# A recurrence and a top-1 mixture of experts on one core: weight loads spread over the first scatters, two chunks in the first routing group, throttles kept in the planner alone

## The chip, the cores and the metric

One core of a Trainium2 chip runs the whole program. The metric is the device time in microseconds (us) of one execution, lower is better. Three runs of the kernel before gave 561.56, 562.37 and 565.24 us, the median is 562.37 us.

## The reference

The inputs are `x` and `f_logit`, both (4, 5056, 256) in float32, a vector `lower_bound` of 256, eight expert embeddings and the two weight matrices of eight experts. First a gated recurrence runs along the 5056 steps of each of the four sequences; then each of the 20224 rows that come out goes to the one expert whose embedding is nearest, and is scaled by that expert's probability.

```python
sig = 1.0 / (1.0 + np.exp(-f_logit))
f = lower_bound + (1.0 - lower_bound) * sig
h = f[:, t] * h + (1.0 - f[:, t]) * x[:, t]      # for each step t; y[:, t] = h
...
logits = xn @ en.T / tau                          # xn, en: rows divided by their norms
expert_idx = np.argmax(logits, axis=1)
out[mask] = gate_w[mask, None] * (np.maximum(y[mask] @ w1[e], 0.0) @ w2[e])
```

## The kernel before, in words

**Stages.** The 20224 rows are cut into 40 chunks of 512 (the last has 256). A chunk is loaded by SP (`load`, L573, three buffers each for `f_logit`, called `fin`, and `x`, called `xin`). `F_` (L774) transposes `fin` on TensorE (L782), ScalarE makes the tanh `th` (L793) and the gate `fg` (L799), once for each half `dh` of the 256 columns. `X_` (L806) transposes `xin` (L816); VectorE multiplies it by the gate (L824) and runs the recurrence as a scan along the row (L840), into `hb`. `Y_` (L847) squares it and turns it back into rows in the tile `Yt`, in chunks below 14 by TensorE transposes (L886) and a copy (L897), later by a bf16 copy `hbf` (L861) and a DMA transpose.

**Routing.** Chunks are put into groups (`groups`, L767): before, chunks 0 and 1 are a group each, then two chunks each up to chunk 37, then 38 and 39 alone; 22 groups. `route_` (L934) computes the logits of a group on TensorE (L945, L949), copies them (L961), transposes them (L967), and a string of small VectorE operations (L976 to L1042) finds the expert and, with some matmuls (L1013 to L1026), the row's slot in a table sorted by expert. `gate_` (L1048) computes the probability with some fifteen more small VectorE operations (L537 to L1095). Both strings are as long for a group of one chunk as for a group of two (with one chunk a memset, L1001, comes on top). Then GpSimd (POOL) scatters the rows, 128 at a time, into the DRAM tensor `XsScratch` (L1109): four indirect DMAs for each chunk, 158 in all.

**Experts.** After some groups `update_` (L1123) writes a table that says which 256 rows of one expert a tile takes (`ups`, L1524: a list of group numbers). `tile_` (L1318) computes one of 81 tiles: it loads the rows, runs the first matmuls (L1434, 32 weight blocks from `wall` in SBUF at a register's address), ReLU on ScalarE and VectorE (L1455, L1460) into `hT`, the second matmuls (L1482), scales the two halves (L1497 on ScalarE, L1501 on VectorE, into `osb`, six buffers) and writes them with two indirect DMAs from POOL (L1507). A tile's matmuls wait for all weights that it might need: tiles 0 to 3 for the loads 0 to 7, tiles 4 to 7 for 0 to 11, the others for all 16 (`FEW`, L397, and `wr`, L1419).

**Weights.** `wload` (L751) asks from POOL for one of 16 loads, 1 MB in float32 read and 512 KB in bf16 written, two for each expert. A load waits until the load two before it has landed. All 16 are handed to the planner with chunk 0 and its priority (L1557).

**Order.** Nothing is ordered by hand. `Prog.op` (L62) records each operation with an engine, a cost, and its dependences: `deps` become semaphore waits where another engine or a DMA is concerned, `order` only places one after the other on an engine. `Prog.schedule` (L129) then plays a list schedule with these costs and writes down one fixed order for each engine; `resolve` (L290) and `emit` put in the waits. Lower `prio` goes first: a chunk's work has the chunk's number, a tile's 10000 and more, so that tiles fill the places in which the plan sees TensorE free. PSUM's eight banks are given out by the same plan (`Hold`). Some dependences are no data dependences but throttles: `F_`'s transposes wait (`deps`, L790) for the readers of `th` and of the same `fg` buffer two chunks ago, `X_`'s transposes read `fg` by their record (L822), though they touch only `xin` and a bank; likewise `Y_`, the logits, the turned rows of the first tiles and the first matmuls list the readers of a buffer that a later copy will write. In the planner VectorE may hold a long operation back for up to 250 ns when an operation of an early chunk is about to be ready (`soon`, L192, for priorities up to 3). The ReLUs carry the tag `mid`; with all routing work planned, the second matmuls that read them are planned 2600 ns later. A scatter and the writes of all but the last four tiles are `paced`: POOL waits for a TensorE step that the plan saw done by then.

```python
if o.dma is not None:
    bus = max(bus, free[e]) + o.nbytes / self.DMA_RATE      # the plan's DMA: one bus in order
    o.end = max(bus, free[e]) + self.DMA_FIX
```

Of the kernel before, what the change touches and what calls it, by code (L numbers as in the profile page):

```python
# [17 lines left out]
class Op:  # L18
    __slots__ = (
        "eng", "fn", "deps", "order", "dma", "val", "know", "used", "cost", "nbytes", "prio",  # L20
        "idx", "start", "end", "tag", "astart", "aend", "hold", "quiet", "late", "paced",
# [13 lines left out]
class Prog:  # L35
# [26 lines left out]
    def op(self, eng, fn, cost, r=(), w=(), x=(), deps=(), order=(), dma=None, nbytes=0, prio=None, tag="", chain=True, h=None):  # L62
# [52 lines left out]
        o.deps, o.order = list(need.values()), list(order.values())  # L115
        self.ops.append(o)
        return o

    def filler(self, q, n):
        f = Op()  # L120
        f.eng, f.dma, f.nbytes, f.cost = "pe", None, 0, n * self.UNIT
        f.val, f.know, f.used, f.tag = 0, None, False, ""
        f.prio, f.idx, f.quiet, f.late, f.paced, f.hold = -9, len(self.ops), True, False, False, ()
        f.deps, f.order = [self.warm_on], []
        f.fn = lambda e: self.warm(e, q, n)
        self.ops.append(f)
        return f

    def schedule(self, first, caps):  # L129
# [3 lines left out]
        for o in self.ops:  # L133
            left[id(o)] = len(o.deps) + len(o.order)
            for d in o.deps:
                succ[id(d)].append((o, True))
            for d in o.order:
                succ[id(d)].append((o, False))
# [34 lines left out]
        while True:  # L173
# [17 lines left out]
            if e == "dve" and avail[e] and avail[e][0][2].cost > 400:  # L191
                soon = min(  # L192
                    (w for w in wait[e] if w[0] <= s + 250 and w[1] < avail[e][0][0] and w[1] <= 3),
                    default=None, key=lambda w: w[:3],
                )
# [177 lines left out]
def bass_hgrn_recurrence__then__cosine_router_kernel(  # L373
# [41 lines left out]
    with ExitStack() as es:  # L415
# [335 lines left out]
        def wload(i, c):  # L751
# [6 lines left out]
            else:  # L758
# [4 lines left out]
                deps=[pr.writer.get(("w", i - 2))], nbytes=1 << 20, prio=c,  # L763
            )


        groups = [[0], [1]] + [[2 * g, 2 * g + 1] for g in range(1, (NCH - 2) // 2)] + [[NCH - 2], [NCH - 1]]  # L767
# [6 lines left out]
        def F_(c):  # L774
            q, nb = c % NXI, nof(c) // P
            n = nof(c)
            for dh in range(DT):
                h = Hold("a")

                def fn(e, dh=dh, h=h):  # L780
# [9 lines left out]
                    deps=[pr.readers.get(("th", dh), []), pr.readers.get(("fg", c % 2, dh), [])],  # L790
# [15 lines left out]
        def X_(c):  # L806
# [4 lines left out]
            for dh in range(DT):  # L811
# [10 lines left out]
                pe(fn, 110 * nb, r=[("xin", q), "ident", ("fg", c % 2, dh)], h=h)  # L822
# [24 lines left out]
        def Y_(c):  # L847
# [32 lines left out]
            for hf in range(nb // 2):  # L880
                h = Hold("a")

                def fn(e, hf=hf, h=h):
# [10 lines left out]
                    deps=pr.readers.get(("Yt", bi % NY, k_, hf), []),  # L894
# [39 lines left out]
        def route_(g):  # L934
# [7 lines left out]
            def lg(e):  # L942
# [13 lines left out]
                lg, 1760, h=hl, deps=pr.readers.get(("lgS", g % 2), []),  # L956
# [361 lines left out]
        def tile_(j, u, g, n):  # L1318
# [57 lines left out]
            if j < NPE:  # L1376
                hy = Hold("a")

                def turn(e):
# [14 lines left out]
                    deps=pr.readers.get(("ys", qy, 0), []), prio=EVP(pr.prio),  # L1394
# [29 lines left out]
            for mp in range(2):  # L1424
                hh = (Hold("m"), Hold("m"))

                def mm1(e, mp=mp, hh=hh):
# [20 lines left out]
                    mm1, 1000 if last else 874, r=yk + wr, h=hh, order=[prev],  # L1448
                    deps=pr.readers.get(("hT", qh, 2 * mp), []) + pr.readers.get(("hT", qh, 2 * mp + 1), []),
                )  # L1450
                for m, h in ((2 * mp, hh[0]), (2 * mp + 1, hh[1])):
                    o = hT[qh][:, 2 * m : 2 * m + 2, :].rearrange("p f c -> p (f c)")
                    if m % 2 == 0:
                        act(
                            lambda e, o=o, h=h: e.activation(o, bank[h.b][:], AF.Relu), 512,  # L1455
                            h=h, w=[("hT", qh, m)], prio=EVP(pr.prio), tag="mid",
                        )
                    else:
# [4 lines left out]
                            512, h=h, w=[("hT", qh, m)], prio=EVP(pr.prio), tag="mid",  # L1463
# [10 lines left out]
            for m in range(4):  # L1474
                if split:
                    at = [(kf, m // 2) for kf in range(4 * (m % 2), 4 * (m % 2) + 4)]
                else:
                    at = [(kf, s) for kf in (2 * m, 2 * m + 1) for s in range(2)]
# [45 lines left out]
        ups = [3, 4, 5, 7, 9, 11, 13, 15, 17, 18, 19, 20] + [NG - 1, NG - 1]  # L1524
# [10 lines left out]
        YBOOST = 1.5  # L1535

# [12 lines left out]
        for c in range(NCH):  # L1549
# [6 lines left out]
            if c == 0:  # L1556
                for i in range(2 * E):  # L1557
                    wload(i, c)
            if c == 1:
                late_constants()  # L1560
            if c in last_of:
# [3 lines left out]
                if g == batches[bi][-1]:  # L1565
                    gate_(bi)
                for u, at in enumerate(ups):
                    if at == g:
                        update_(u, g, u == len(ups) - 1)
# [63 lines left out]
```

## Time and profile before

| | us |
|---|---|
| median of three runs (561.56 to 565.24) | 562.37 |
| the profiled execution | 565.46 |
| its span, first to last instruction | 563.7 |
| TensorE (PE) busy | 475.2 |
| VectorE (DVE) busy | 359.5 |
| GpSimd (POOL) busy | 331.9 |
| ScalarE (ACT) busy | 321.1 |

The span's share that an engine is busy is a mean over stages with different limits. PE is the matmuls, PEld the loads of their stationary side, which overlap with them. POOL's busy time is the issue of indirect DMAs, nearly 1 us each, and leaves out 0.3 us between one and the next. "PEclk" is the clock that was granted to TensorE, as a share of full speed. The DMA share is a mean over 16 engines and comes out a little over 1 where all are busy.

### The profile page before, as it was taken

To read this page: it belongs to the slowest core of one execution; us is meant where nothing else is said; L and a number is where in the kernel's file an instruction comes from. 1 tells how busy PE (TensorE), PEld (TensorE's weight loads), DVE (VectorE), ACT (ScalarE), POOL (GpSimd) and SP (SyncE) were. 2 spreads that over 40 slices of the span, in tenths; PEclk is the share of its full clock that TensorE was granted. 3 is DMA by queue.
4 is the path that set the end of the run, shared out by engine and by line. 5 is a ranking of instruction groups with operands and counts; after the bars stand their busy time and mean duration, and the time that the engine had idled before them with its cause. 6 is when DMAs were issued, how large, how long until landed. Compare 5 with 4: busy or idle time off the path is not lost. (4 is left out here: it accounts for less than half of the span.)

```text
span 563.7 us, 12407 instructions
## 1 busy us (share of the span) xinstructions
PE 475.2 (84%) x4106; PEld 382.8 (68%) x4106; DVE 359.5 (64%) x1075; ACT 321.1 (57%) x573; POOL 331.9 (59%) x388
## 2 busy tenths in 40 slices
PE   7796778979798789887887988888988897978994
PEld 4474557757577567656765657777777776867894
DVE  7869978877787667875877876533444343443452
ACT  4878768877787566757776753333333332333342
POOL 6164565655665565564666665656665666655555
PEclk8969988998998889999999999999999999999998
DMA  8999999999999788879896543353343433444422
GB/s 243 302 311 313 318 254 311 287 254 219 206 234 241 202 205 190 238 172 219 221 241 133 117 92 99 113 127 105 100 110 95 110 88 100 106 109 101 106 65 74
DMA packets 119681, 100.49 MB, mean 178 GB/s; under 512 B 96884, under 2 KB 98687, under 8 KB 119616
## 3 DMA queue, kind: packets, MB, share of 16 engines
q1 hardware_dynamic: 101664, 59.38, 42.5%
q0 software_dynamic: 16224, 40.26, 26.2%
q8 instruction: 36, 0.59, 0.5%
q10 hardware_dynamic: 1728, 0.01, 0.2%
q14 instruction: 29, 0.24, 0.2%
HBM read 59.21 MB, written 32.93 MB: 163 GB/s over the span
## 5 line engine op out<-in xcount | busy, mean ns | idle before, releaser
L1507 POOL DMA_INDIRECT out_dram<-osb,xm x162 | 160.7, 992 | 107.6 <-issue 34.0
L1109 POOL DMA_INDIRECT XsScratch<-Yt,sli x158 | 152.2, 963 | 105.6 <-issue 26.6
L1434 PE MATMUL bank<-ys,wall 128*128 128x256 bf16 (+1 forms) x1392 | 174.4, 271 | 19.1 <-issue 13.4
L1482 PE MATMUL bank<-wall,hT 128*128 x1296 | 172.8, 274 | 15.0 <-issue 12.6
L1460 DVE TENSOR_SCALAR hT<-bank 128x512 bf16<-128x512 f32 x162 | 108.4, 684 | 100.8 <-remote 46.0
L1434 PEld LDWEIGHTS bank<-ys,wall 128*128 x1392 | 147.5, 145 | 34.9 <-issue 24.7
L1455 ACT ACTIVATE hT<-bank 128x512 bf16<-128x512 f32 x162 | 94.0, 597 | 114.1 <-remote 49.5
L1482 PEld LDWEIGHTS bank<-wall,hT 128*128 128x128 bf16 x1296 | 124.4, 98 | 42.9 <-issue 23.0
L840 DVE TENSOR_TENSOR_SCAN hb<-fg,hb,bank 128x512 f32<-128x512 f32 (+4 forms) x78 | 95.9, 1236 | 0.1
L1501 DVE TENSOR_SCALAR osb<-bank,xm 128x256 f32<-128x256 f32 x81 | 38.8, 479 | 59.7 <-ACT osb L1497 32.6
L1497 ACT ACTIVATE osb<-bank,xm 128x256 f32<-128x256 f32 x81 | 38.4, 475 | 59.7 <-remote 17.4
L816 PE MATMUL bank<-ident,xin 128*128 128x128 f32 x316 | 53.2, 294 | 22.7 <-ACT fg L799 12.9
L799 ACT ACTIVATE fg<-th,cs 128x512 f32<-128x512 f32 (+1 forms) x80 | 64.4, 812 | 1.4 <-DVE cs L627 0.2
L816 PEld LDWEIGHTS bank<-ident,xin 128*128 128x128 f32 x316 | 37.7, 149 | 34.6 <-ACT fg L799 16.9
L824 DVE SCALAR_TENSOR_TENSOR bank<-fg,bank 128x512 f32<-128x512 f32 (+1 forms) x80 | 54.1, 680 | 9.6 <-PE bank L816 6.8
L793 ACT ACTIVATE th<-bank 128x512 f32<-128x512 f32 (+1 forms) x80 | 46.3, 592 | 22.7 <-PE bank L782 14.2
L782 PE MATMUL bank<-ident,fin 128*128 128x128 f32 x316 | 53.5, 300 | 4.5 <-DMA fin<-in_f_logit_dram 2.0
L782 PEld LDWEIGHTS bank<-ident,fin 128*128 128x128 f32 x316 | 40.4, 155 | 12.2 <-issue 4.5
L852 ACT ACTIVATE sq<-hb 128x1024 f32<-128x1024 f32 (+1 forms) x40 | 41.8, 1045 | 2.0 <-DVE hb L840 1.6
L945 PE MATMUL bank<-hb,eT 128*8 128x512 f32 (+1 forms) x160 | 41.7, 599 | 0.3 <-issue 0.3
L949 PE MATMUL bank<-sq,onesf 128*1 128x512 f32 (+1 forms) x160 | 41.5, 597 | 0.0
L861 ACT ACTIVATE hbf<-hb 128x512 bf16<-128x512 f32 x50 | 31.4, 629 | 4.7 <-DVE hb L840 4.2
(139 smaller groups left out, 305.3 us busy)
## 6 DMA issues: line engine op xcount, KB each, us to landing
fin<-in_f_logit_dram SPq DMA_DIRECT2D x39, 512.0 KB
xin<-in_x_dram SPq DMA_DIRECT2D x39, 512.0 KB
wall<-in_moe_w_dram POOLq DMA_DIRECT2D x16, 512.0 KB, 10.6
out_dram<-osb,xm POOLq DMA_INDIRECT x162
XsScratch<-Yt,sli POOLq DMA_INDIRECT x158
ys<-XsScratch SPq DMA_TRANSPOSE x81
xm<-XsScratch SPq DMA_DIRECT2D x75, 2.0 KB
osb<-XsScratch SPq DMA_DIRECT2D x6, 136.0 KB
```

The lines of the kernel that those rows point to most:

```text
L782: i = e.transpose(bank[h.b][:, b : nb * P : nb], fin[q][:, b, dh * P : (dh + 1) * P], ident[:],)
L793: lambda e, dh=dh, h=h: e.activation(th[dh][:, 0:n], bank[h.b][:, 0:n], AF.Tanh, scale=0.5),
L799: lambda e, dh=dh: e.activation(fg[c % 2][:, dh, 0:n], th[dh][:, 0:n], AF.Identity, bias=cs[:, dh, 0:1], scale=cs[:, dh, 1:2],),
L816: i = e.transpose(bank[h.b][:, b : nb * P : nb], xin[q][:, b, dh * P : (dh + 1) * P], ident[:],)
L824: lambda e, dh=dh, h=h: e.scalar_tensor_tensor(out=bank[h.b][:, 0:n], in0=fg[c % 2][:, dh, 0:n], scalar=1.0, in1=bank[h.b][:, 0:n], op0=AL ...
L840: lambda e, dh=dh, s0=s0, s1=s1, init=init, h=h: e.tensor_tensor_scan(hb[c % NH][:, dh, s0:s1], fg[c % 2][:, dh, s0:s1], bank[h.b][:, s0:s ...
L1109: lambda e, j=o + j, i=o + k_ * 4 + b: e.indirect_dma_start(out=Xs[:, :], out_offset=bass.IndirectOffsetOnAxis(ap=sli[y][:, j : j + 1], axis=0
L1434: i = e.matmul(bank[hh[f // 2].b][:, at : at + R_], wall[:, bass.ds(a1[j, s][(4 * mp + f) * DT + kt] - WA - WREV, 2 * FT * P),].bitcast(BF ...
L1455: lambda e, o=o, h=h: e.activation(o, bank[h.b][:], AF.Relu), 512,
L1460: lambda e, o=o, h=h: e.tensor_scalar(o, bank[h.b][:], 0.0, None, op0=ALU.max),
L1482: i = e.matmul(po(s), hT[qh][:, kf, s * P : (s + 1) * P], wall[:, bass.ds(a2[j, s if last else 0][kf] - WA, 2 * D)].bitcast(BF16), start=( ...
L1507: lambda e, s=s: e.indirect_dma_start(out=out[:, :], out_offset=bass.IndirectOffsetOnAxis(ap=xm[qx][:, s, 1:2], axis=0), in_=osb[qo][:, s, :],
```

## The change

Six edits. (1) `op` takes a list `behind`: the planner counts it like `deps`, but no semaphore wait comes of it. The throttles named above move from `deps` to `behind`, and `X_`'s transposes no longer record `fg` as read. (2) Chunks 0 and 1 form one group; there are 21 groups, and `ups` is renumbered to the same chunks. (3) Six weight loads stay with chunk 0; the other ten are handed over two by two after the groups that end with chunks 3, 5, 7, 9 and 11, each ordered on POOL behind that group's last scatter. (4) `soon` takes priorities up to 5. (5) For the last two tiles the tag `mid` is gone, and the last tile's second half of first matmuls is ordered behind the second matmuls of the tile before. (6) The last tile's second matmuls alternate between its two halves instead of finishing the first half first.

```diff
         o.deps, o.order = list(need.values()), list(order.values())
+        o.behind = [q for q in flat(behind) if q is not o]
...
-            left[id(o)] = len(o.deps) + len(o.order)
-            for d in o.deps:
+            left[id(o)] = len(o.deps) + len(o.order) + len(o.behind)
+            for d in o.deps + o.behind:
                 succ[id(d)].append((o, True))
...
-                    (w for w in wait[e] if w[0] <= s + 250 and w[1] < avail[e][0][0] and w[1] <= 3),
+                    (w for w in wait[e] if w[0] <= s + 250 and w[1] < avail[e][0][0] and w[1] <= 5),
...
                 deps=[pr.writer.get(("w", i - 2))], nbytes=1 << 20, prio=c,
+                order=[pr.writer.get(("Xs", gof[c][0]))],
...
-        groups = [[0], [1]] + [[2 * g, 2 * g + 1] for g in range(1, (NCH - 2) // 2)] + [[NCH - 2], [NCH - 1]]
+        groups = [[2 * g, 2 * g + 1] for g in range((NCH - 2) // 2)] + [[NCH - 2], [NCH - 1]]
...
-                    deps=[pr.readers.get(("th", dh), []), pr.readers.get(("fg", c % 2, dh), [])],
+                    behind=[pr.readers.get(("th", dh), []), pr.readers.get(("fg", c % 2, dh), [])],
...
-                pe(fn, 110 * nb, r=[("xin", q), "ident", ("fg", c % 2, dh)], h=h)
+                pe(fn, 110 * nb, r=[("xin", q), "ident"], h=h, behind=[pr.writer[("fg", c % 2, dh)]])
...
-                    deps=pr.readers.get(("Yt", bi % NY, k_, hf), []),
+                    behind=pr.readers.get(("Yt", bi % NY, k_, hf), []),
...
-                lg, 1760, h=hl, deps=pr.readers.get(("lgS", g % 2), []),
+                lg, 1760, h=hl, behind=pr.readers.get(("lgS", g % 2), []),
...
-                    deps=pr.readers.get(("ys", qy, 0), []), prio=EVP(pr.prio),
+                    behind=pr.readers.get(("ys", qy, 0), []), prio=EVP(pr.prio),
...
-                    mm1, 1000 if last else 874, r=yk + wr, h=hh, order=[prev],
-                    deps=pr.readers.get(("hT", qh, 2 * mp), []) + pr.readers.get(("hT", qh, 2 * mp + 1), []),
+                    mm1, 1000 if last else 874, r=yk + wr, h=hh,
+                    order=[prev, last_mm[2] if mp and n == NM - 1 else None],
+                    behind=pr.readers.get(("hT", qh, 2 * mp), []) + pr.readers.get(("hT", qh, 2 * mp + 1), []),
...
-                            h=h, w=[("hT", qh, m)], prio=EVP(pr.prio), tag="mid",
+                            h=h, w=[("hT", qh, m)], prio=EVP(pr.prio), tag="mid" if n < NM - 2 else "",
...
-                    at = [(kf, m // 2) for kf in range(4 * (m % 2), 4 * (m % 2) + 4)]
+                    at = [(kf, m % 2) for kf in range(4 * (m // 2), 4 * (m // 2) + 4)]
...
-        ups = [3, 4, 5, 7, 9, 11, 13, 15, 17, 18, 19, 20] + [NG - 1, NG - 1]
+        ups = [2, 3, 4, 6, 8, 10, 12, 14, 16, 17, 18, 19] + [NG - 1, NG - 1]
...
+        WBEHIND = [(6, 1), (8, 2), (10, 3), (12, 4), (14, 5)]
...
             if c == 0:
-                for i in range(2 * E):
+                for i in range(WBEHIND[0][0]):
                     wload(i, c)
...
+                for n, (i0, at) in enumerate(WBEHIND):
+                    if at == g:
+                        for i in range(i0, WBEHIND[n + 1][0] if n + 1 < len(WBEHIND) else 2 * E):
+                            wload(i, c)
```

## Rows read from the trace of the kernel before

**Rows 1.** The page's slices: 40 equal parts of the span, busy tenths.

```profile
PE   7796778979798789887887988888988897978994
...
DVE  7869978877787667875877876533444343443452
...
DMA  8999999999999788879896543353343433444422
```

**Rows 2.** Stretches: PE, PEld, DVE, ACT, POOL busy us (instructions); PEclk, DMA share, GB/s.

```profile
48.00:94.00 46.00, 36.41 (x304) 27.11 (x303) 40.48 (x143) 35.73 (x58) 28.73 (x33) 0.89 1.02 296
94.00:108.00 14.00, 12.05 (x126) 9.72 (x124) 10.54 (x38) 11.71 (x23) 9.00 (x11) 1.00 1.08 280
108.00:333.00 225.00, 191.31 (x1665) 147.08 (x1664) 170.24 (x520) 159.91 (x282) 133.63 (x137) 0.97 0.85 205
333.00:490.00 157.00, 137.54 (x1171) 118.04 (x1170) 72.02 (x206) 55.75 (x113) 96.81 (x99) 1.00 0.39 102
490.00:553.00 63.00, 57.59 (x586) 51.71 (x584) 25.88 (x45) 22.58 (x46) 35.75 (x37) 1.00 0.42 98
```

**Rows 3.** TensorE in order of time (start, us, instruction): chunk 4, the first tile.

```profile
28.71 1.09 PE L816 MATMUL bank<-ident,xin 128*128 128x128 f32 x4 [1.99 <-DMA xin<-in_x_dram]
...
94.02 1.91 PE L1434 MATMUL bank<-ys,wall 128*128 128x256 bf16 x16
```

**Rows 4.** POOL in order of time: the last six writes, first and last.

```profile
553.80 0.98 POOL L1507 DMA_INDIRECT out_dram<-osb,xm  x1 [2.27 <-DVE osb L1501]
...
560.26 0.98 POOL L1507 DMA_INDIRECT out_dram<-osb,xm  x1 [0.30 <-issue]
```

**Rows 5.** VectorE in order of time, the first two routing rounds.

```profile
20.19 0.16 DVE L976 TENSOR_REDUCE rmax<-bank 128x4 f32<-128x32 f32 x1
...
22.67 0.19 DVE L1035 TENSOR_TENSOR slt<-bank,oh 128x32 f32<-128x32 f32 x1 [0.27 <-PE bank L1026]
...
23.31 0.69 DVE L824 SCALAR_TENSOR_TENSOR bank<-fg,bank 128x512 f32<-128x512 f32 x1
...
26.76 0.19 DVE L1035 TENSOR_TENSOR slt<-bank,oh 128x32 f32<-128x32 f32 x1 [0.58 <-PE bank L1026]
...
27.64 1.27 DVE L840 TENSOR_TENSOR_SCAN hb<-fg,hb,bank 128x512 f32<-128x512 f32 x1
...
29.12 0.14 DVE L1095 TENSOR_SCALAR Yt<-tokf 128x4 int32<-128x4 f32 x1
```

**Rows 6.** POOL in order of time: weight loads (L762) and scatters (L1109).

```profile
27.50 1.06 POOL L1109 DMA_INDIRECT XsScratch<-Yt,sli  x1 [6.94 <-DVE rs L1062]
...
45.30 0.58 POOL L762 DMA_DIRECT2D wall<-in_moe_w_dram  x1 [4.37 <-DMA wall<-in_moe_w_dram]
47.41 1.00 POOL L1109 DMA_INDIRECT XsScratch<-Yt,sli  x1 [1.52 <-DVE Yt L1095]
...
59.09 0.99 POOL L1109 DMA_INDIRECT XsScratch<-Yt,sli  x1 [0.63 <-PE bank L886]
...
101.14 0.58 POOL L762 DMA_DIRECT2D wall<-in_moe_w_dram  x1
...
122.13 0.96 POOL L1109 DMA_INDIRECT XsScratch<-Yt,sli  x1 [0.30 <-PE bank L816]
```

**Rows 7.** Groups: count, busy us, mean ns, idle us before them and what ended it.

```profile
L824 DVE SCALAR_TENSOR_TENSOR bank<-fg,bank 128x512 f32<-128x512 f32 (+1 forms) x80 | 54.1, 680 | 9.6 <-PE bank L816 6.8
```

**Rows 8.** TensorE's group of L816 from 48 to 108 us.

```profile
L816 PE MATMUL bank<-ident,xin 128*128 128x128 f32 x72 | 13.3, 315 | 9.9 <-ACT fg L799 9.1 <-issue 0.8
```

**Rows 9.** TensorE's groups from 108 to 333 us.

```profile
L1434 PE MATMUL bank<-ys,wall 128*128 128x256 bf16 x446 | 60.7, 283 | 7.3 <-issue 3.6 <-DVE osb L1501 2.4 <-DVE slt L1035 1.0
L816 PE MATMUL bank<-ident,xin 128*128 128x128 f32 x191 | 30.2, 281 | 8.7 <-ACT th L793 3.1 <-ACT fg L799 2.3 <-ACT hT L1455 1.8
L782 PE MATMUL bank<-ident,fin 128*128 128x128 f32 x184 | 29.7, 286 | 2.1 <-DVE hb L840 1.0 <-issue 0.8 <-DVE nr L1058 0.2
```

More of the change, by code (lines that the diff above doesn't have):

```diff
@@ L20 @@
         "eng", "fn", "deps", "order", "dma", "val", "know", "used", "cost", "nbytes", "prio",
-        "idx", "start", "end", "tag", "astart", "aend", "hold", "quiet", "late", "paced",
+        "idx", "start", "end", "tag", "astart", "aend", "hold", "quiet", "late", "paced", "behind",
     )
@@ L60, in __init__, with op @@
         self.asked = {}
-    def op(self, eng, fn, cost, r=(), w=(), x=(), deps=(), order=(), dma=None, nbytes=0, prio=None, tag="", chain=True, h=None):
+    def op(self, eng, fn, cost, r=(), w=(), x=(), deps=(), order=(), dma=None, nbytes=0, prio=None, tag="", chain=True, h=None, behind=()):
         o = Op()
@@ L123, in filler @@
         f.prio, f.idx, f.quiet, f.late, f.paced, f.hold = -9, len(self.ops), True, False, False, ()
-        f.deps, f.order = [self.warm_on], []
+        f.deps, f.order, f.behind = [self.warm_on], [], []
         f.fn = lambda e: self.warm(e, q, n)
@@ L1462, in tile_ @@
                             ),
-                            512, h=h, w=[("hT", qh, m)], prio=EVP(pr.prio), tag="mid",
+                            512, h=h, w=[("hT", qh, m)], prio=EVP(pr.prio), tag="mid" if n < NM - 2 else "",
                         )
```

## The prediction

> **What bounds the kernel now.** I read the page's slices first, then busy time by stretch, then what each engine waited for. The slices show no engine full from end to end: PE is at 7 to 9 tenths nearly everywhere, DVE is high only in the first half, the DMA engines are at 9 for the first third and at 3 to 4 late [rows 1]. So the span is cut where the limits change [rows 2].
>
> Up to 94 us there is no expert work: the first tile's matmuls begin at 94.02 [rows 3]. From 48 to 94 DVE is busy for 40.48 of 46 us (88%), PE for 36.41 (79%), and the DMA share is 1.02: scans and small routing operations set the pace, with transfers close behind. At 28.71 PE had waited 1.99 us for chunk 4 of `x` [rows 3].
>
> From 108 to 333 us chunks and tiles are mixed. PE is busy for 191.31 of 225 us (85%), DVE for 76% [rows 2]. POOL's indirect DMAs come at best every 1.29 us: the last six start from 553.80 to 560.26, five steps in 6.46 us [rows 4]. Its 137 instructions thus take 177 us, 79%. PE is nearest to its limit and loses 34 us.
>
> From 333 to 490 late scatters run beside the tiles: 99 POOL instructions take 128 of 157 us, PE 137.54. From 490 to 553 PE is at 57.59 of 63 [rows 2]. Then six writes go out back to back.
>
> **The change, part by part.** The sum is made against the profiled execution: 565.46 us, of which 1.76 lie outside the span of 563.7. It was 3.09 us above the median of 562.37, and that is taken off at the end.
>
> *One group fewer.* From 20.19 to 29.26 (29.12 + 0.14) DVE works on the routing of chunks 0 and 1, 9.07 us. Take out a product of 0.69, a scan of 1.27 and waits of 0.27 and 0.58: 6.26 us, 3.1 a round [rows 5]. One round goes, and chunk 2's second scan, at 27.64, stands right behind them. Against it: chunk 0's scatters now wait for the joint round. If that ends where the second did, at 29.26, the first scatter slips from 27.50 by 1.76 us; POOL had idled 6.94 us there [rows 6]. And chunk 4 cannot come before its data, at 28.71. Ends: a loss of 1.8 and a gain of 3.1. I take a gain of 2.0, nearer to the DVE rows, since DVE is the fuller engine there.
>
> *Throttles without a semaphore.* `X_`'s transposes (L816) no longer wait for `fg`. Early, this is worth what DVE loses by it: its product waited 6.8 us for these transposes in the whole run [rows 7], though PE waited 9.1 us for `fg` from 48 to 108 alone [rows 8]. Not all of the 6.8 is due to the gate. Ends 0 and 6.8; I take 3.0.
>
> From 108 to 333 PE is the fuller engine, and its own time counts: 3.1 + 2.3 + 1.8 before L816 and 1.0 before L782, 8.2 us [rows 9]. Late next are the same gate before DVE's product, then a free bank, then the copy of the logits, a data dependence that stays. And ACT now waits itself for DVE's scan two chunks back before it overwrites `fg`; behind it queue the tanh, the ReLUs and the output copies, and PE's second matmuls wait for these. PE's 1.0 us before L782 paid for that. So the lower end is a loss of 1.0, as that wait changes engine; the upper 8.2. I take half, 4.0. The throttles between two steps of PE itself (logits, first matmuls, turned rows) are no waits on the chip: 0. The one before L886 stands in none of the rows as a wait for a scatter: 0, up to 1.
>
> *Weight loads.* The number of issues is the same, so their cost is 0; what moves is the place. The load at 45.30 is the eighth; it goes behind the 16th scatter, now at 59.09, and the last, at 101.14, behind the 48th, now at 122.13 [rows 6]. POOL's wait of 4.37 us for a landing before 45.30 goes. But the scatter behind it still waited, until 47.41, for DVE's last step of the gate [rows 6]: that covers it, and should DVE come 3 us earlier, up to 3 of it would count. The first four tiles need the eighth load, tiles from the ninth on the last: 446 matmuls of sixteen for a tile are 28 tiles in 225 us, 8 us each [rows 9], so the ninth begins some 64 us after the first, near 158. No tile should wait. The transfers move from 40 to 100 us into 60 to 130, where the DMA share is 1.02 to 1.08 [rows 2]. Ends: a loss of 7.5 (rival C) and a gain of 3.0. I take 0: of L816's 9.9 us of idle time from 48 to 108 all is put down to the gate and to issue, and from 108 to 333 only 1.5 us of its 8.7 and 0.1 of L782's 2.1 are left that could be a wait for data [rows 8, 9]. The chunk loads have slack.
>
> All kinds of transfers, asked for by SP and by POOL, share the 1.02 to 1.08. The Trainium skill ("DMA: Bandwidth & Descriptors", section "Issuing engines are not separate DMA queues") says that transfers of any engine end up on the same 16 DMA engines and interleave. By that rule a load asked for later is not hidden, it meets other transfers; if all of it counted the sum would be rival C's. The trace agrees that the engines are full there, and does not show who would be late.
>
> *Order and tail.* `soon` lets other small DVE operations of chunks 4 and 5 go first, and the whole plan is made anew. No row prices that: 0, with 3.1, one routing round, to both sides. At the end POOL waits 2.27 us before its last six writes [rows 4]. With the last tiles' second matmuls planned earlier part of that goes, but the last tile's first half is finished later. Ends 0 and 2.27; I take 0.7.
>
> *Sum.* The early gains, 2.0 + 3.0 = 5.0, bring the first tile forward. The chunk loads, with three buffers each and full DMA engines, do not all follow; I pass on 0.6 of it, 3.0. With 4.0 and 0.7 that is 7.7. 565.46 - 7.7 = 557.76, less 3.09: **554.7 us**.
>
> **Rivals.** A measurement of this kernel can tell about 1%, 5.6 us: below 556.7 is faster, above 568.0 slower.
>
> *B, the wait only moves.* PE comes earlier and stands before the next step in its order, and full DMA engines eat the early gain. Left are 0.7 at the end and 0.5 early: 564.26 - 3.09 = 561.2. For it: no engine is at its limit, so the chain counts and not one engine's waits. Against it: 3.1 us of DVE work really go. The same comes out if the change does not do what it says, because the new plan puts the loads and transposes where the old one had them.
>
> *C, slower: the moved loads hit the chunk loads.* Some four of the ten moved loads fall behind 94 us that did not lie there. At 280 GB/s [rows 2] 512 KB take 1.87 us, four of them 7.5. If the chunk loads come that much later, chunks and tiles do too, and the throttles' gain is lost to data that is not there: 565.46 + 7.5 - 3.09 = 569.9. It decides from where PE's waits for `fin` and `xin` between 90 and 140 us come to more than 5 us. For it: the DMA share. Against it: the slack above.
>
> *D, all of it counts.* 3.1 + 6.8 + 8.2 + 2.27 = 20.4: 545.06 - 3.09 = 542.0. Against it: DVE and the DMA engines are nearly full early.
>
> **How the numbers follow.** My sum (A) has 0.48, B 0.27, C 0.18, D 0.07. A's own range is 549 to 560. Faster by over 1%: 0.41 of A, all of D, 0.03 of B: 0.51. Within 1%: 0.07 of A, 0.22 of B, 0.03 of C: 0.32. Slower: 0.15 of C, and 0.02 of B for a plan that falls badly: 0.17. The range, 545 to 569, leaves out D, half of C and little else.
>
> **What would show it.** Right: 21 routing rounds; chunk 2's second scan near 25 us and the first tile near 90; no wait of L816 for ScalarE's gate, and PE's idle time from 108 to 333 down by some 4 us; POOL not waiting for a landed load behind 31 us; less than 2.27 us before the last six writes. Wrong: the first tile at 94 or later though the waits are gone (B); waits of over 5 us for `fin` or `xin` (C); or a tail behind the last scan that is longer than now, which no term touches.

## The result, and the profile after

Ten runs of the kernel after gave 566.52 to 574.51 us with a median of 569.1, ten of the kernel before 560.39 to 567.62 with a median of 564.74. The recorded ratio is 1.0111, with a 95% interval of 1.0079 to 1.0143 (the two medians alone give 1.008): slower by about 1%, where 554.7 us was forecast. The profiled execution took 570.37 us, its span is 568.5.

The change did what it says. The ten loads go out in pairs. POOL in order of time, kernel after (start, us, engine, line, operation; in brackets the idle time before it and what ended it):

```profile
27.25 0.71 POOL L763 DMA_DIRECT2D wall<-in_moe_w_dram  x1 [6.46 <-DMA wall<-in_moe_w_dram]
31.03 0.55 POOL L763 DMA_DIRECT2D wall<-in_moe_w_dram  x1 [3.07 <-DMA wall<-in_moe_w_dram]
56.74 1.37 POOL L763 DMA_DIRECT2D wall<-in_moe_w_dram  x2
...
125.36 1.37 POOL L763 DMA_DIRECT2D wall<-in_moe_w_dram  x2
```

The waits for ScalarE's gate are gone. The groups of TensorE's `xin` transposes (L816 before, L818 after), first from 48 to 108 us, to be held against [rows 8], then from 108 to 333 us, against [rows 9]:

```profile
L818 PE MATMUL bank<-ident,xin 128*128 128x128 f32 x64 | 10.3, 293 | 1.1 <-DVE bank L826 1.1
```

```profile
L818 PE MATMUL bank<-ident,xin 128*128 128x128 f32 x192 | 29.9, 279 | 3.6 <-issue 3.6
```

And the first tile is 3.1 us earlier, 90.87 instead of 94.02 [rows 3]:

```profile
90.87 2.79 PE L1436 MATMUL bank<-ys,wall 128*128 128x256 bf16 x24
```

So far this is the forecast. The table by stretch is where it parts. Kernel after, the stretches of [rows 2], same columns (PE, PEld, DVE, ACT, POOL busy us with instructions; PEclk, DMA share, GB/s):

```profile
48.00:94.00 46.00, 34.35 (x301) 26.61 (x302) 37.91 (x144) 36.82 (x61) 25.40 (x28) 0.89 0.93 255
94.00:108.00 14.00, 12.76 (x125) 10.24 (x124) 10.90 (x32) 11.42 (x21) 9.38 (x11) 1.00 0.85 264
108.00:333.00 225.00, 186.11 (x1677) 145.76 (x1676) 172.48 (x541) 159.23 (x279) 134.88 (x139) 0.98 0.89 212
333.00:490.00 157.00, 135.96 (x1131) 118.33 (x1130) 70.06 (x183) 54.88 (x110) 96.58 (x99) 0.96 0.39 100
490.00:553.00 63.00, 54.71 (x529) 48.30 (x528) 24.39 (x42) 21.61 (x42) 36.36 (x37) 0.97 0.39 96
```

Look at POOL's column. From 48 to 94 us it gets 28 instructions done where it did 33 before; then 11 as before, 139 for 137, 99 as before and 37 as before. By 94 us it has done 96 in all where it had done 101. Three of these five are weight loads, which the change itself puts later (12 are out by then, before it was 15); two are scatters (32 for 34). By 553 us, with all loads long out, it is two behind (380 for 382). At 1.29 us a step [rows 4] that is 2.6 us of the 4.8 by which the span grew. TensorE made more of its matmuls from 108 to 333 us (1677 for 1665) and fewer later (1131 for 1171, 529 for 586): work was brought forward and the time given back.

All of the loss lies ahead of the last scan, which ends at 332.3 before and at 338.2 after; from there to the end of the span it is 231.4 us before and 230.3 after. The last scan, before and after:

```profile
331.57 0.73 DVE L840 TENSOR_TENSOR_SCAN hb<-fg,hb,bank 128x256 f32<-128x256 f32 x1
```

```profile
337.48 0.74 DVE L842 TENSOR_TENSOR_SCAN hb<-fg,hb,bank 128x256 f32<-128x256 f32 x1
```

The gates show where the early gain goes. The gate of chunks 2 and 3 ends at 43.0 instead of 47.1 us and that of chunks 4 and 5 at 58.6 instead of 62.8, both 4.1 us earlier. The gate of chunks 6 and 7 is 2.7 us later (73.0 for 70.3), that of chunks 8 and 9 6.2 us later (92.7 for 86.5). Before, VectorE's last step of the gate of chunks 8 and 9, and the first scatter of chunk 8 on POOL:

```profile
86.41 0.12 DVE L1095 TENSOR_SCALAR Yt<-tokf 128x8 int32<-128x8 f32 x1
```

```profile
92.43 0.99 POOL L1109 DMA_INDIRECT XsScratch<-Yt,sli  x1 [1.19 <-DVE hb L840]
```

POOL was still busy with chunk 7 when that gate ended, and 6 us lay between. Now there is no such reserve. Where POOL stood still up to 94 us, kernel after:

```profile
70.02 1.37 POOL L763 DMA_DIRECT2D wall<-in_moe_w_dram  x2
74.41 1.01 POOL L1111 DMA_INDIRECT XsScratch<-Yt,sli  x1 [3.01 <-DVE tbl L1257]
...
86.92 1.37 POOL L763 DMA_DIRECT2D wall<-in_moe_w_dram  x2
94.46 1.01 POOL L1111 DMA_INDIRECT XsScratch<-Yt,sli  x1 [6.16 <-DVE nr L544]
```

The 6.16 us stand before the first scatter of chunk 8, which waits for two things. One is the gate of chunks 8 and 9, which VectorE ends at 92.7 us. The other is its pacing, here the first matmuls shown above, which end at 93.66 (90.87 + 2.79): this is the wait that ended last, by 0.9 us. VectorE in that gate's last steps, kernel after:

```profile
91.07 0.23 DVE L978 TENSOR_REDUCE rmax<-bank 128x8 f32<-128x64 f32 x1 [3.50 <-PE bank L969]
...
91.81 0.20 DVE L1088 RECIPROCAL Yt<-den 128x8 f32<-128x8 f32 x1
91.94 0.69 DVE L1463 TENSOR_SCALAR hT<-bank 128x512 bf16<-128x512 f32 x1
92.55 0.17 DVE L1097 TENSOR_SCALAR Yt<-tokf 128x8 int32<-128x8 f32 x1
```

A tile's ReLU (L1463) and the next group's routing (L978, which itself waited 3.50 us for TensorE) stand inside that gate: the plan gives VectorE one fixed list, and in the new one the gate's last steps come behind a step of the next group that was not ready. These 3.50 us are VectorE's longest wait between the gate before and this one; in the kernel before the longest was 2.30 us.

### The profile page after: what moved, and what is told of

Same layout as the page of the kernel before. It is cut to its first block, busy times and chain, and to the rows that moved or that the text cites. A ratio compares the mean times of both kernels' runs of the same rounds, so it can differ in the third digit from the quotient of the medians.

```text
span 568.5 us, 12341 instructions
## 1 busy us (share of the span) xinstructions
PE 466.6 (82%) x4100; PEld 381.6 (67%) x4100; DVE 359.4 (63%) x1049; ACT 322.4 (57%) x571; POOL 332.5 (58%) x388
## 5 line engine op out<-in xcount | busy, mean ns | idle before, releaser
L1436 PEld LDWEIGHTS bank<-ys,wall 128*128 x1392 | 149.6, 146 | 42.6 <-issue 23.7
L1463 DVE TENSOR_SCALAR hT<-bank 128x512 bf16<-128x512 f32 x162 | 108.0, 685 | 96.4 <-PE bank L1436 31.5
L842 DVE TENSOR_TENSOR_SCAN hb<-fg,hb,bank 128x512 f32<-128x512 f32 (+4 forms) x78 | 96.1, 1237 | 0.2
L1504 DVE TENSOR_SCALAR osb<-bank,xm 128x256 f32<-128x256 f32 x81 | 38.9, 481 | 76.0 <-ACT osb L1500 50.4
L784 PE MATMUL bank<-ident,fin 128*128 128x128 f32 x316 | 50.0, 283 | 10.3 <-DMA fin<-in_f_logit_dram 6.7
L818 PE MATMUL bank<-ident,xin 128*128 128x128 f32 x316 | 50.4, 287 | 4.7 <-issue 3.6
L784 PEld LDWEIGHTS bank<-ident,fin 128*128 128x128 f32 x316 | 37.8, 146 | 17.0 <-DMA fin<-in_f_logit_dram 4.6
L818 PEld LDWEIGHTS bank<-ident,xin 128*128 128x128 f32 x316 | 38.0, 147 | 12.9 <-issue 11.8
```

Source lines behind the costliest of these rows:

```text
L784: i = e.transpose(bank[h.b][:, b : nb * P : nb], fin[q][:, b, dh * P : (dh + 1) * P], ident[:],)
L818: i = e.transpose(bank[h.b][:, b : nb * P : nb], xin[q][:, b, dh * P : (dh + 1) * P], ident[:],)
L842: lambda e, dh=dh, s0=s0, s1=s1, init=init, h=h: e.tensor_tensor_scan(hb[c % NH][:, dh, s0:s1], fg[c % 2][:, dh, s0:s1], bank[h.b][:, s0:s ...
L1436: i = e.matmul(bank[hh[f // 2].b][:, at : at + R_], wall[:, bass.ds(a1[j, s][(4 * mp + f) * DT + kt] - WA - WREV, 2 * FT * P),].bitcast(BF ...
L1463: lambda e, o=o, h=h: e.tensor_scalar(o, bank[h.b][:], 0.0, None, op0=ALU.max),
```

## The experiments

Times differ by chip, so each ratio is to the kernel before on the same chip. e5 to e8 and e17 and e18 ran on two chips on which the kernel before took 474.3 and 471.5 us instead of 564 to 570; more on that at the end. The kernel after itself was not run on these two. The ratios are the recorded ones; quotients of the medians differ from them by up to 0.6%.

**The waits.** `e1_after_waits`: all orders as after, but what stands in `behind` for another engine is a semaphore wait again.

```diff
-        o.behind = [q for q in flat(behind) if q is not o]
+        o.behind = [q for q in flat(behind) if q is not o]; o.deps += [q for q in o.behind if (q.eng != eng or q.dma) and id(q) not in need]; o.behind = [q for q in o.behind if not (q.eng != eng or q.dma)]
```

> The changed kernel with its order of instructions untouched on all five engines, and the throttles sent to the chip as semaphore waits again. Theory P (the new order, not the missing waits, makes it slower): 569 to 574 us, the same as the changed kernel or some us slower, since the waits cost PE time. Theory Q (without the waits PE runs into banks and buffers too early): 562 to 566 us, as before or better.

Measured: 576.74 us, ratio 1.0126 (1.0081 to 1.0171). By the ratio as slow as after: it is not the missing waits.

`e2_before_nowaits`: all orders as before; the throttle waits before L782, L816 and L886 are taken out of the finished plan.

```diff
-        self.out = out
+        self.out = [(setattr(o, 'deps', [d for i, d in enumerate(o.deps) if i >= o.skip[1] or id(d) not in o.skip[0]]), o)[1] for o in out]
```

> The kernel before, same order on all five engines, with the throttle waits of the chunk transposes (L782, L816, L886) left out. Theory P: 560 to 565 us, the gain of 4 us or less that the waits before L816 and L782 are worth on PE from 108 to 333 us, or nothing. Theory Q: 568 us or more.

Measured: 569.21 us, ratio 0.9987 (0.9956 to 1.0018). The waits that the prediction priced at 7 us are worth 0.7 us by themselves, 2.5 at most. They did go: TensorE's group of L816 from 108 to 333 us, kernel e2, has 1.4 us of idle time left of 8.7 [rows 9]. But TensorE did 1657 matmuls there, not more than the 1665 of before: it stood elsewhere instead.

```profile
L816 PE MATMUL bank<-ident,xin 128*128 128x128 f32 x188 | 29.0, 277 | 1.4 <-issue 0.5 <-DVE slt L1035 0.3 <-ACT th L793 0.3
```

**The tail.** `e3_after_oldtail` undoes edits 5 and 6 in after, `e4_before_newtail` makes them alone in before.

```diff
-                    order=[prev, last_mm[2] if mp and n == NM - 1 else None],
+                    order=[prev],
...
-                    at = [(kf, m % 2) for kf in range(4 * (m // 2), 4 * (m // 2) + 4)]
+                    at = [(kf, m // 2) for kf in range(4 * (m % 2), 4 * (m % 2) + 4)]
```

> The changed kernel with edits 5 and 6 (the last two tiles' tag, the order and the alternation of the last tile) undone; the order differs only at the end. Theory T (the end was made worse): 564 to 567 us, 2.5 to 4.5 us below the changed kernel, with the last six writes starting earlier. Otherwise 568 to 570 us.

> The kernel before with edits 5 and 6 alone; the order differs only at the end. Theory T: 567 to 569 us. My prediction's term for the end: 0.7 us less than before, 564. Otherwise within 1 us of before, 564 to 566.

Measured: 577.61 us, 1.0131 (1.0076 to 1.0186), and 573.43 us, 1.0060 (1.0027 to 1.0092). Undone, the tail gives nothing back; done alone, it costs. After itself does not pay this price: its last six writes start with a wait of 1.11 us. The price in e4 can be seen at POOL: two of the six writes that went out back to back in [rows 4] now come 5.68 us after the others.

```profile
562.30 0.98 POOL L1507 DMA_INDIRECT out_dram<-osb,xm  x1 [0.30 <-issue]
568.98 0.98 POOL L1507 DMA_INDIRECT out_dram<-osb,xm  x1 [5.68 <-DVE osb L1501]
570.26 0.98 POOL L1507 DMA_INDIRECT out_dram<-osb,xm  x1 [0.31 <-issue]
```

**Groups and loads, each alone** (on a chip with 474.3 us before). `e5_before_group` is before with edit 2, `e6_before_weights` before with edit 3, `e7_after_weights0` after with edit 3 undone, `e8_after_groups` after with edit 2 undone.

```diff
# e7_after_weights0
-        WBEHIND = [(6, 1), (8, 2), (10, 3), (12, 4), (14, 5)]
+        WBEHIND = [(16, -1)]
# e8_after_groups
-        groups = [[2 * g, 2 * g + 1] for g in range((NCH - 2) // 2)] + [[NCH - 2], [NCH - 1]]
+        groups = [[0], [1]] + [[2 * g, 2 * g + 1] for g in range(1, (NCH - 2) // 2)] + [[NCH - 2], [NCH - 1]]
```

> The kernel before with edit 2 alone: chunks 0 and 1 in one group, the list of updates renumbered to the same chunks. Theory G (the shared group is what brings the slower order): ratio to before 1.006 to 1.015, POOL's first scatter after 30 us instead of at 27, and the write of tile 56 some 3 us or more after that of before. Theory W (the spread weights bring it): 0.995 to 1.003 here. Theory N (no single edit does; any new plan of this kernel lands anywhere within about 1% of before): a ratio on either side, without relation to the other three runs of this call.

> The kernel before with edit 3 alone: ten weight loads two by two behind the scatters of chunks 3, 5, 7, 9 and 11. Theory W: ratio 1.006 to 1.015, with waits of TensorE for chunk loads (L783) between 45 and 140 us of over 5 us in sum, or a write of tile 56 that is 3 us or more late. Theory G: 0.995 to 1.003. Theory N: either side.

> The kernel after with edit 3 undone: all sixteen weight loads are asked for with chunk 0. Theory W: the loss of 1.1% goes, ratio 0.997 to 1.003 to before. Theory G: it stays, 1.008 to 1.015. Theory N: either, and not the complement of the run with edit 3 alone.

> The kernel after with edit 2 undone: chunks 0 and 1 a group each, as before. Theory G: the loss goes, 0.997 to 1.003 to before, and the gate of chunks 8 and 9 ends by 87 us instead of 92.7. Theory W: it stays, 1.008 to 1.015. Theory N: either, and not the complement of the run with edit 2 alone.

Measured: e5 1.0021 (0.9972 to 1.0069), e6 1.0159 (1.0105 to 1.0213), e7 0.9958 (0.9910 to 1.0007), e8 1.0153 (1.0060 to 1.0245). All four fall where theory W has them, or just beside it: with the loads spread the kernel is slower, with all of them at chunk 0 it is not, whatever the groups. In e6 part of the reason is rival C's: TensorE waits for a chunk of `x` behind the last pair of loads, and POOL's next write with it (TensorE's row first, then POOL's):

```profile
127.22 1.09 PE L817 MATMUL bank<-ident,xin 128*128 128x128 f32 x4 [5.33 <-DMA xin<-in_x_dram]
```

```profile
114.12 1.37 POOL L762 DMA_DIRECT2D wall<-in_moe_w_dram  x2
...
129.18 0.99 POOL L1508 DMA_INDIRECT out_dram<-osb,xm  x1 [5.91 <-PE bank L817]
```

In e8, as slow and with the loads spread, no such wait of over 0.3 us stands between 45 and 140 us, nor in after's own trace on the chip with 565 us. C's wait is real in e6, but it is not what made these two slow; for e8 the reason stays open.

**The loads' place on POOL, with nothing else moved.** `e9_before_poolmove` keeps before's plan and moves the loads 6 to 15 on POOL to where the change has them; `e10_after_poolback` keeps after's plan and moves them back.

```diff
-        self.out = out
+        self.out = move(out, {6: 16, 7: 16, 8: 24, 9: 24, 10: 32, 11: 32, 12: 40, 13: 40, 14: 48, 15: 48})
...
+def move(out, at):     # load k behind the at[k]-th scatter
```

> The kernel before with the orders of TensorE, VectorE, ScalarE and SP as they were; on POOL alone the weight loads 6 to 15 are moved two by two behind the 16th, 24th, 32nd, 40th and 48th scatter, where the change put them. Theory H (the loads filled holes in POOL's queue in which it had no scatter to issue; moved behind scatters they cost POOL time of their own, and POOL decides the end): ratio 1.004 to 1.010, POOL's idle time beyond 0.3 us a step in 50 to 100 us 3 us or more above that of before, and four loads instead of one after 100 us. Theory O (only the new order of the other engines costs): 0.997 to 1.003.

> The kernel after with its orders on all engines, but on POOL the weight loads 6 to 15 stand behind as many scatters as in the kernel before (8, 8, 11, 15, 16, 20, 24, 28, 32, 38). Theory H: at least half of the 1.1% goes, ratio 0.996 to 1.005. Theory O: 1.008 to 1.015, as after.

Measured: e9 562.90 us, 0.9994 (0.9961 to 1.0027), e10 573.08 us, 1.0152 (1.0081 to 1.0222). Theory H falls at both ends: the place on POOL is worth nothing. What is left is the order that the planner wrote for the other engines.

**Less work for POOL.** `e11_before_nowrite` and `e12_after_nowrite` leave out the 16 writes of eight tiles; those rows of the output are not written.

```diff
+    drop = [o for o in out if o.dma is not None and o.dma[:2] == "od"]
+    drop = {id(o) for o in drop[60:76]}
```

> The kernel before, its orders unchanged, with the 16 writes of eight tiles (the 31st to the 38th in POOL's order) left out; the output lacks those tiles. Sixteen issues of 0.99 us with 0.30 between are 20.6 us of POOL. Theory B (POOL's backlog behind the routing sets the end): 8 to 20 us faster, and the lag of the writes behind the second matmuls at tiles 54 to 66 falls from 17 us to under 8. Theory E (TensorE alone sets it): 0 to 3 us faster.

> The kernel after, its orders unchanged, with the same 16 writes left out. Theory B: it gains more than the kernel before does by the same step, and ends level with it or earlier, since its first 32 tiles were some 3 us earlier: the two differ by under 0.4%, and the lag at tiles 54 to 66 falls from 21 us to under 10. Theory E: it stays 0.8 to 1.5% behind that kernel.

Measured: 554.40 us, 0.9847 (0.9787 to 0.9907), and 557.66 us, 0.9877 (0.9810 to 0.9944). Of 20.6 us of POOL's work 8.6 (0.0153 of 563.9) come off the end, so POOL's queue is on the path for part of the way; what holds the rest was not told apart. The two kernels are then 0.3% apart by the ratios, as theory B has it, and 0.6% by the medians, of four runs each with intervals of 1.2 to 1.3%: this does not decide. The other half of B was wrong: the writes still lag by 16 and 21 us behind their matmuls at tiles 54 to 59.

**VectorE's order mended by hand.** `e13_after_gatefirst` changes VectorE's list alone, at the two gates; `e14_after` is after itself beside it.

```diff
-        self.out = out
+        self.out = gates_first(out)     # what is not needed for the gate goes behind it, on VectorE alone
```

> The kernel after with one engine's order changed at two places: on VectorE the two gate products and the scan of chunk 10 that stood inside the gate of chunks 6 and 7, and a product and a scan of chunk 13, two ReLUs and the first routing steps of chunks 10 and 11 that stood inside the gate of chunks 8 and 9, come right behind these gates; the other engines keep their orders. Theory V (that stretch of VectorE holds up POOL, and POOL's idle time there comes out at the end): POOL's idle time beyond 0.3 us a step in 50 to 100 us falls from some 15 to 9 to 12 us, and the kernel is 0.5 to 1.0% faster than after on the same chip. Theory L (the loss comes later, from tiles that go ahead of chunks): within 0.3% of after.

> The kernel after as it is, on the same chip as the other three. All theories: ratio to before 1.006 to 1.015, POOL's idle time in 50 to 100 us 13 to 16 us.

Measured: e13 583.19 us, 1.0218 (1.0153 to 1.0282), e14 578.15 us, 1.0136 (1.0086 to 1.0186). Theory V expected a gain, and none came (the two intervals overlap). The gate of chunks 8 and 9 ended at 92.1 (92.7 in after's profile, 96.1 in e14's, an execution of 584.28 us). But POOL's scatter then waited until 99.37. Kernel e13, POOL, then TensorE:

```profile
88.30 1.37 POOL L763 DMA_DIRECT2D wall<-in_moe_w_dram  x2
99.37 1.00 POOL L1111 DMA_INDIRECT XsScratch<-Yt,sli  x1 [9.70 <-DVE nr L546]
```

```profile
94.05 4.51 PE L1436 MATMUL bank<-ys,wall 128*128 128x256 bf16 x24 [3.02 <-DVE hb L842]
98.40 0.60 PE L1485 MATMUL bank<-wall,hT 128*128 x4
```

The scatter is paced by the first matmuls of a tile, as in after, and these now waited 3.02 us for the scan that had been moved back, and took 4.51 instead of 2.79 us. Two waits stood side by side, the gate at 92.7 and the paced step at 93.7 in after. The paced step ended last there already, so an earlier gate could gain nothing, and what was moved behind the gate made that step later.

**Edit 4 alone, and edit 3 undone once more.** `e15_before_soon5` and `e16_after_weights0` on the chip of e13.

```diff
-                    (w for w in wait[e] if w[0] <= s + 250 and w[1] < avail[e][0][0] and w[1] <= 3),
+                    (w for w in wait[e] if w[0] <= s + 250 and w[1] < avail[e][0][0] and w[1] <= 5),
```

> The kernel before with edit 4 alone: VectorE may be held for operations up to priority 5 instead of 3. Theory S (holding VectorE for the gates of chunks 4 and 5 pushes work of later chunks into the gates behind them): POOL's idle time in 50 to 100 us rises by 3 us or more and the ratio is 1.004 to 1.012. Theory N (edit 4 is nothing by itself): 0.997 to 1.003 and idle time within 1.5 us.

> The kernel after with edit 3 undone, as in an earlier run, now on the chip of this call. If the spread loads are what brings the slower order: 0.992 to 1.002 to before, and 1% or more faster than after. If the earlier gain was that chip's alone: 1.005 to 1.015.

Measured: e15 572.27 us, 1.0052 (1.0016 to 1.0089), e16 573.22 us, 1.0082 (1.0054 to 1.0110). Edit 4 alone does what theory S has: the gate of chunks 4 and 5 ends earlier (57.0 for 62.8 in before), and those of chunks 6 and 7 (81.2 for 70.3) and 8 and 9 (95.5 for 86.5) later, the same pattern as in after. POOL in e15:

```profile
73.10 0.74 POOL L762 DMA_DIRECT2D wall<-in_moe_w_dram  x1
82.22 0.98 POOL L1109 DMA_INDIRECT XsScratch<-Yt,sli  x1 [8.38 <-PE bank L886]
```

e16 came out between its two theories: undoing the spread of the loads gives back some 0.5% here (573.22 against 578.15, with intervals that overlap), not all. It is the same program as e7: 0.4% faster than before on that chip and 0.8% slower on this one. So what a new order costs depends on the chip too.

**The pacing left out,** in after (`e17_after_nopace`) and in before (`e18_before_nopace`), on the chip with 471.5 us.

```diff
-                        o.deps.append(past[-1])
+                        pass
```

> The kernel after with the orders of all engines as they are and the pacing's waits left out: POOL's scatters and writes wait for their data alone. Theory Pc (the pacing turns TensorE's delay against the plan into POOL's idle time): POOL's idle time beyond 0.3 us a step in 50 to 100 us falls from some 15 to under 12 us, that of 100 to 500 us from some 85 to under 50, and the ratio to before is 0.98 to 1.005. Theory St (the rows are late, and the later pauses are not TensorE's doing): idle time within 2 us in 50 to 100 and within 15 in 100 to 500 us, ratio 1.008 to 1.016.

> The kernel before with its orders and without the pacing's waits. Theory Pc: idle time in 50 to 100 us 8 to 10 us as before, since TensorE is nearer to its plan there; later pauses fewer; ratio 0.98 to 1.0, and the gap to the run of after without pacing under 0.5%. Theory St: 0.997 to 1.003, and the gap stays at 0.8 to 1.5%.

Measured: e17 482.02 us, 1.0205 (1.0151 to 1.0259), e18 471.38 us, 1.0003 (0.9972 to 1.0034). Without pacing before is the same, and after still loses: 2.05%, against 1.1 to 1.4% with pacing on other chips. Its scatter at the gate of chunks 8 and 9 (ended at 91.8) still waits, now for its rows alone, and starts 0.3 us behind that gate.

```profile
82.38 1.37 POOL L763 DMA_DIRECT2D wall<-in_moe_w_dram  x2
92.10 1.00 POOL L1111 DMA_INDIRECT XsScratch<-Yt,sli  x1 [8.35 <-DVE best L994]
```

So the rows are late, as theory St has it, though the ratio lies above its 1.016. e17's profile, of an execution of 484.80 us, also has two waits of TensorE for `xin`, 2.85 and 2.73 us, between 120 and 132 us; rival C's test, over 5 us, is met there, and how much of the ratio they make was not told apart. St's second half, on the pauses between 100 and 500 us, could not be tried on this chip, which does not have them. The gates moved forward and the pacing left out together were not tried.

**All of them on one scale.** The number of instructions that POOL had done by 150 us, from the table by stretch of each run's profile, against the ratio:

| chips with 564 to 570 us before | by 150 us | ratio |
|---|---|---|
| e2 waits out of before | 137 | 0.9987 |
| before | 136 | 1 |
| e9 loads moved on POOL alone | 136 | 0.9994 |
| e4 tail alone | 136 | 1.0060 |
| after | 134 | 1.0111 |
| e16 after, loads at chunk 0 | 134 | 1.0082 |
| e15 edit 4 alone | 133 | 1.0052 |
| e10 after, loads back on POOL | 133 | 1.0152 |
| e1 after, waits back | 133 | 1.0126 |
| e3 after, old tail | 132 | 1.0131 |
| e14 after once more, profiled at 584.28 us | 131 | 1.0136 |
| e13 after, gates first | 130 | 1.0218 |

| chips with 471 to 475 us before | by 150 us | ratio |
|---|---|---|
| e18 before, no pacing | 148 | 1.0003 |
| e7 after, loads at chunk 0 | 146 | 0.9958 |
| e5 group alone | 145 | 1.0021 |
| e6 loads alone | 141 | 1.0159 |
| e8 after, old groups | 138 | 1.0153 |
| e17 after, no pacing | 134 | 1.0205 |

Two of the rows behind it, before and e13:

```profile
0.00:150.00 150.00, 121.52 (x980) 92.34 (x980) 121.17 (x404) 113.13 (x187) 85.09 (x136) 0.91 1.01 278
```

```profile
0.00:150.00 150.00, 112.41 (x954) 86.14 (x954) 116.34 (x361) 111.03 (x183) 79.32 (x130) 0.95 0.96 263
```

On the first chips a kernel that has POOL two to six instructions behind at 150 us is 0.5 to 2.2% slower, whichever edit put it there. e4 is the exception: its price is at the end. One kernel can differ by three between two profiles (after 134, e14 131), so the order within the table says little. On the other chips the link is looser: e5 is three behind e18 and e7 two, and neither is slower beyond its interval. Nor is the count one thing: before's 136 hold 58 scatters and 10 writes, after's 134 hold 54 and 12, so part of the scatters' delay is POOL's own new order. The tables show that the two go together, not which causes which. That POOL's queue is the path was shown in part, by e11; TensorE is nearly full late too, and what each of the two holds there was not told apart.

## Why the prediction was wrong

**What bounds the kernel: failed, and this failed first.** "PE is nearest to its limit and loses 34 us" from 108 to 333 us, so waits taken off PE were counted as time. They were not on the path: without the throttle waits (e2) the kernel gains 0.7 us. In after, PE's idle time in that stretch did not fall by some 4 us, it rose from 33.7 to 38.9. The engine that the sum set aside is POOL, "79%". Its 21% there are short gaps, which TensorE has on that chip as well; on a chip where these are missing, POOL has no gap left. Kernel e5, 150 to 300 us, on the chip with 474.3 us: 118 instructions at 1.27 us are 150 us of 150.

```profile
150.00:300.00 150.00, 147.36 (x1404) 122.43 (x1402) 141.56 (x497) 123.84 (x223) 113.92 (x118) 1.00 1.01 239
```

TensorE is as full there, 147.36 us. POOL issues 320 indirect DMAs and 16 loads one by one, and a scatter that it cannot issue early, for want of rows, costs its 1.27 us later. So when the scatters' rows are ready was a quantity to forecast beside when TensorE may run. That POOL sets the pace on the chips with 564 to 570 us is argued; e11 shows it for part of the way.

**One group fewer (+2.0 us): the scan came as said, the time did not.** Chunk 2's second scan, the sixth on VectorE, starts at 22.61 instead of 27.64 [rows 5], earlier than the forecast's 25 us. But the next thing in line pays for it: the joint round starts only at 26.66, behind chunk 3's first scan, and chunk 3's second scan stands inside its gate. Kernel after, the sixth and the eighth scan and the end of the gate:

```profile
22.61 1.28 DVE L842 TENSOR_TENSOR_SCAN hb<-fg,hb,bank 128x512 f32<-128x512 f32 x1
...
30.50 1.28 DVE L842 TENSOR_TENSOR_SCAN hb<-fg,hb,bank 128x512 f32<-128x512 f32 x1
...
32.05 0.12 DVE L1097 TENSOR_SCALAR Yt<-tokf 128x8 int32<-128x8 f32 x1
```

The gate ends at 32.17, not at 29.26, and the first scatter slips by 5.95 us to 33.45, where 1.76 was the bound. The next two gates are 4.1 us earlier all the same, and that is lost again by the gate of chunks 6 and 7. Edit 2 alone, on the chip with 474.3 us, gives 1.0021 (0.9972 to 1.0069).

**Throttles (+3.0 and +4.0 us): the waits went as said, the time did not.** L818 has no wait for ScalarE left in either stretch. The price was TensorE's idle time, and e2 puts it at a gain of 0.7 us (0.0013 of 570), by its interval between a loss of 1.0 and a gain of 2.5. This is the largest mis-sized term of the sum.

**Weight loads (0, bounds -7.5 to +3.0): the lower bound held where it was measured alone.** e6 loses 7.5 us by its ratio (0.0159 of 474.3) and 4.8 by its median; that the first equals C's bound is luck, as C's wait is 5.33 us of it. On the chips with 564 to 570 us the loads cost nothing as a place on POOL (e9), as the prediction said, and edit 3 alone was not run; with it undone after is some 0.5% better (e16). The prediction saw only the place: the planner counts a load's transfer, and with ten of them gone from the front it writes another order for TensorE, VectorE, ScalarE and SP. The Trainium skill's rule ("DMA: Bandwidth & Descriptors", section "Issuing engines are not separate DMA queues"), that transfers of any engine interleave on the same DMA engines, agrees with e6's 5.33 us; after's own trace shows no such wait.

**Order and tail (0, with 3.1 to both sides, and +0.7): the step that turned a missing gain into a loss.** With after's order the kernel is by the ratios 1.1 to 1.5% slower than the same chip's before, also with the waits, the tail or the loads' place put back (after, e1, e3, e10, e14): 6 to 9 us, at least twice the bound. Edit 4 alone costs 0.5%, 3.0 us. The tail edits alone cost 0.6%, 3.4 us, where a gain was taken, though in after itself they cost nothing that can be seen. Nothing in the new order was waited for longer in the trace of before, so no row could price it; the bound of one routing round had no ground. Which of its many moves costs what stays open beyond edit 4.

**Rivals.** C's 569.9 us lies beside the measured 569.1, but by its own test (over 5 us of waits for chunk loads from 90 to 140 us) it did not happen in that run, so the match is luck. B, that the wait only moves, is nearest to what did: the early gain of 3.1 us at the first tile is there, and POOL's wait for scatters, 6.16 us, takes its place. B priced that as no loss; the prediction's 0.02 "for a plan that falls badly" is what came.

**What would have shown it:** none of the three signs of being wrong came. The first tile was early, no wait for `fin` or `xin` of over 0.3 us stood from 45 us on, and the tail behind the last scan was no longer than before. All signs of being right came but one, PE's idle time from 108 to 333 us. So the signs watched TensorE, the loads and the end, and the loss lay between them: a sign on when each gate ends, or when POOL issues each scatter, would have shown it.

## What to carry to other kernels

Ask which engines have a fixed list of issues that cannot be made shorter, and forecast when each can start its own; idle time taken off another engine may be worth next to nothing, here 0.7 of 7.0 us. In a kernel whose order is written by a planner, an edit to a cost, a priority or a hand-over date is an edit to every engine's order: price it by running each edit alone and the finished order with one thing put back, since no row of the old trace holds it. And when a wait is moved, look for a second one that ends within a microsecond of it.

## What was not expected of the hardware

The same kernel took 564 to 570 us on some chips and 471.5 and 474.3 us on two others. In the records the difference is short gaps, most of them of half a microsecond to two, on every engine. From 150 to 300 us POOL did 91 instructions and TensorE 1102 matmuls in the kernel before, whose row stands here; on the chip with 474.3 us e5, which differs in edit 2 alone, did 118 and 1404 (its row stands above).

```profile
150.00:300.00 150.00, 127.54 (x1102) 98.22 (x1103) 112.03 (x337) 105.80 (x185) 88.17 (x91) 0.97 0.87 212
```

The granted clock does not explain it: 0.97 and 1.00, both at or near its upper level of 2.4 GHz. What the gaps are stays open. The two chips differ by a sixth of the time, and the gaps made POOL look as if it had room.
